# Two more raw heads loaded into an idle buffer at the start, and the first tail load moved behind the weights

## The chip, the cores and the metric

The kernel runs on one core of one Trainium2 chip. The metric is the device time of one execution in microseconds (us), the median of three runs. Three float32 modules are fused: block-causal attention, a gated two-layer block ("MoE 1") and a gated block that also mixes along the sequence ("MoE 2").

## The reference

```python
scores = 1/sqrt(64) * (q @ k.T); mask to blocks of 64: block_i >= block_j      # B=4, H=8, S=576, D=64
attn = softmax(scores);  x = attn @ v, heads side by side                      # (4, 576, 512)

xk, xr = mu*x + (1-mu)*x_prev  (one mu each; x_prev is x one step earlier)
x = sigmoid(xr @ w_r) * (relu(xk @ w_k)**2 @ w_v)                              # d_ff 1024

h = gelu(x @ w_in);  u, v = halves of h
x + (u * (w_sg @ layernorm(v) + b_sg)) @ w_out
```

## The kernel before

The function `fused_kernel` records operations on tiles; nothing is emitted while it runs. `Plan.schedule` then plays the recorded list forward several times with a table of durations (`play`, line 464), each time with other priorities, keeps the best play, and `emit` writes every engine's instructions in that order. All emitted instructions therefore carry line 670. A change to one tile or one rule can move instructions on every engine.

**Attention.** It works on 24 units for the first two batches: 16 first-kind units (`"D"`: the first 256 rows of one head, units 0 to 15) and 8 second-kind units (`"H"`: the remaining rows of two heads, units 16 to 23); the other two batches follow in the same way. A unit needs scores (tiles S0, S1, M: `S<-...` on TensorE), the softmax (row minimum and scaling on VectorE, exponential on ScalarE, tile P), transposes of P (tile T), copies of T (PH on ScalarE, PL on VectorE) and products with V (tile O). A first-kind unit loads one raw tile of 320 KB from `low`. A second-kind unit loads two raw tiles of 544 KB from `high` and one "tail" of 352 KB from `tails` (ring `tail`, one buffer), and it moves 64 KB from tile Q to tile q with a DMA (`q<-Q`) before its second score product `S<-k,q`.

**Where raw heads go.** `load` (line 909) takes a tile of `early` for the first units, and after that a tile of the ring `qkv`, which has four buffers (`RAW = 4`) and hands them out in order. `early` (lines 1482, 1483) borrows tiles of MoE 1 that are not yet in use: four heads in `kh`, four in `kl`, two in one buffer of `xh`. Units 10 to 15 go through `qkv`; a buffer of it is also used once for building mask rows. The tile `th` (ring of one) holds the tanh results of MoE 1's first part and stands empty until then.

**MoE 1** runs its products (`M<-xh,wv`: keys, then gates, then values) on TensorE between attention's. Weights arrive as raw 1024 KB tiles in the ring `w` (four buffers) and are converted by ScalarE (`wv<-w`) and VectorE (four operations each) before use; a buffer of `w` is free for the next load when its conversion is done. The first part's products on batch 1 need tile xh_515, whose fourth quarter comes from heads 14 and 15.

**The queue of loads.** SP issues all loads in order. In the planner, line 561 keeps a weight load (tag `w`) off SP while more than 4000 ns of transfers are queued; other loads are issued as they come due.

**Fillers.** Where the planner expects TensorE to idle, it inserts small matmuls on a tile of zeros (`O<-calm`) to keep the clock up; each takes TensorE's time when the gap isn't there.

Of the kernel before, what the change touches and what calls it, by code (L numbers as in the profile page):

```python
# [9 lines left out]
F32 = mybir.dt.float32  # L10
# [13 lines left out]
NL, NH, NT = 640, 1088, 704  # L24
# [40 lines left out]

FILL = 128
BACKLOG = 4000
MORE = 20.0
FILL_DUTY = 1.0
COLD_DUTY = 1.0  # L70
# [262 lines left out]
class Plan:  # L333
# [130 lines left out]
    def play(self, rings):  # L464
# [7 lines left out]
        rings16, lanes = [0.0] * 16, [-40.0] * 8  # L472
# [31 lines left out]
        def zeros(a):  # L504
            calm, op, v = self.filler.alts[0][2]["rhs"], Op(-1), a["out"]
            calm = calm.bitcast(F32) if a["lhsT"].dt == F32 else calm
            op.alts = (("tensor", "matmul", dict(out=v, lhsT=calm[:, 0:v.shape[0]], rhs=calm[:, 0:v.cols], start=False, stop=False)),)
            return op
# [9 lines left out]
        while True:  # L518
            best = None
            for e in soon:  # L520
# [3 lines left out]
                if ripe[e]:  # L524
                    t = free[e]
                elif soon[e]:
                    t = max(free[e], soon[e][0][0])
# [6 lines left out]
            t, e = best  # L534
            while soon[e] and soon[e][0][0] <= t - SLACK[e]:
                _, n, i = heapq.heappop(soon[e])
                heapq.heappush(ripe[e], (self.ops[n].p, n, i))
            if not ripe[e]:
                _, n, i = heapq.heappop(soon[e])
# [7 lines left out]
            _, n, i = heapq.heappop(ripe[e])  # L547
            if e == "PE" and STALL:
# [9 lines left out]
                    heapq.heappush(ripe[e], y)  # L558
                _, n, i = x
            op = self.ops[n]  # L560
            if e == "SP" and max(rings16) - t > BACKLOG and op.tiles and op.tiles[0].args["tag"] == "w":
                heapq.heappush(soon[e], (max(rings16) - BACKLOG, n, i))
                continue
            if e == "DVE" and len(op.alts) > i + 1 and op.alts[i + 1][0] == op.alts[i][0] and lock["POOL"] <= t:
# [20 lines left out]
            elif op.alts[i][1] == "dma_start":  # L585
# [3 lines left out]
                t = max(t, lanes.pop(0) + 40)  # L589
# [8 lines left out]
            else:  # L598
                busy, d, port = takes(e, *op.alts[i][1:])
                if e != "PE":  # L600
                    busy, d = busy + MORE, d + MORE
                s = t
                if e == "PE":
# [3 lines left out]
                    if filler and self.filler_from <= t and gap > (100 if gate.slow else 300):  # L607
                        x = gate.step(free[e])
                        more, n = filler, FILL
                        if opened:  # L610
                            more, n = zeros(group) if group["out"].cols <= FILL else None, 4 * group["out"].cols
# [123 lines left out]
def fused_kernel(ctx: ExitStack, tc: tile.TileContext, low, high, tails, mu,  # L735
# [11 lines left out]
    def pool(name, **kw):  # L747
        p = Pool(plan, name, **kw)
        return p, p
# [66 lines left out]
    mcm, mtile = pool("moe1")  # L816
# [663 lines left out]
        return t  # L1480

    early = [t[:, i] for tag in ("kh", "kl") for t in [mtile([128, 4, NL], F32, tag, 1)] for i in range(4)]
    early += [t[:, i] for tag in ("xh",) for t in [mtile([128, 2, NL], F32, tag, 2)] for i in range(2)]
    for n in range(LD0):
        load(n)
    take(loads, 1)
# [69 lines left out]
    for i, x in moe1():  # L1556
# [5 lines left out]
        i = ready  # L1562
# [328 lines left out]
    for c in range(2):  # L1891
        t = raw[c].rearrange("p (a n) -> p a n", n=HF)
# [128 lines left out]
```

## Time and profile before

| what | us |
|---|---|
| three runs | 655.10, 656.12, 656.96 |
| median | 656.12 |
| the profiled execution | 658.0 |
| its span in the trace | 656.3 |
| TensorE busy in the span | 646.5 (99%) |

The page's busy time of TensorE counts every matmul from its start to its modelled end, so short waits can be hidden in it. The trace answers say, for each engine, what ended its idle time ("waits"), list instructions in order of time ("timeline"), sum busy time in given stretches ("windows") and list DMA issues with the time to landing.

### The profile page before, as it was taken

To read this page: it belongs to the slowest core of one execution; us is meant where nothing else is said; L and a number is where in the kernel's file an instruction comes from. 1 tells how busy PE (TensorE), PEld (TensorE's weight loads), DVE (VectorE), ACT (ScalarE), POOL (GpSimd) and SP (SyncE) were. 2 spreads that over 40 slices of the span, in tenths; PEclk is the share of its full clock that TensorE was granted. 3 is DMA by queue.
4 is the path that set the end of the run, shared out by engine and by line. 5 is a ranking of instruction groups with operands and counts; after the bars stand their busy time and mean duration, and the time that the engine had idled before them with its cause. 6 is when DMAs were issued, how large, how long until landed. Compare 5 with 4: busy or idle time off the path is not lost.

```text
span 656.3 us, 12280 instructions
## 1 busy us (share of the span) xinstructions
PE 646.5 (99%) x4074; PEld 595.7 (91%) x4074; DVE 540.8 (82%) x1454; ACT 463.2 (71%) x1164; POOL 254.2 (39%) x298
## 2 busy tenths in 40 slices
PE   9989999999999999999999999999999999999997
PEld 7978778778999999999999989999898998998997
DVE  4978999988777888785897775784999999789697
ACT  6999877678966999988888976870763744534323
POOL 3033333345722457557454532440205243143054
PEclk9999999999999999999999999999999999999999
DMA  8794521333222344333343002902420440240016
GB/s 338 303 357 128 201 58 54 124 122 103 72 72 82 112 118 142 104 106 99 99 136 110 27 2 98 371 37 64 127 73 0 137 145 1 74 145 1 0 31 196
DMA packets 39615, 74.92 MB, mean 114 GB/s; under 512 B 7040, under 2 KB 22912, under 8 KB 39552
## 3 DMA queue, kind: packets, MB, share of 16 engines
q1 hardware_dynamic: 39408, 74.14, 34.3%
q8 instruction: 32, 0.52, 0.3%
q14 instruction: 31, 0.25, 0.1%
q10 hardware_dynamic: 144, 0.00, 0.0%
HBM read 62.59 MB, written 9.44 MB: 110 GB/s over the span
## 4 chain that ended last, share of the span: by engine, by line
PE 84%; ACT 7%; DMA 3%; DVE 3%; issue 1%; POOL 0%; SPq 0%; POOLq 0%; ACTq 0%; DVEq 0%
PE B L670 29%; PE M L670 26%; PE O L670 11%; PE S L670 10%; PE T L670 9%; ACT P L670 2%; DMA q<-Q 1%; ACT wv L670 1%; DMA kh<-low_dram 1%; DVE P L670 1%; DVE xT L670 1%; DMA x2d<-xh 0%; DMA o<-x2d 0%; ACT Q L670 0%; ACT PH L670 0%
## 5 line engine op out<-in xcount | busy, mean ns | idle before, releaser
L670 DVE TENSOR_TENSOR PL<-T,PH 128x384 fp32r<-128x384 f32 (+1 forms) x128 | 63.4, 504 | 32.3 <-ACT PH L670 23.0
L670 ACT ACTIVATE PH<-T 128x384 fp32r<-128x384 f32 (+3 forms) x152 | 65.8, 434 | 31.4 <-PE T L670 27.1
L670 PE MATMUL M<-xh,w 128*128 128x384 f32 (+1 forms) x272 | 75.7, 340 | 0.0
L670 PE MATMUL M<-xh,wv 128*128 128x256 f32 (+2 forms) x264 | 71.5, 359 | 0.0
L670 DVE TENSOR_SCALAR_CACHE_REDUCE P<-S 128x128 f32<-128x128 f32 (+2 forms) x124 | 58.7, 489 | 15.2 <-PE S L670 8.9
L670 ACT ACTIVATE P<-S,nb 128x128 f32<-128x128 f32 (+2 forms) x124 | 65.7, 538 | 6.4 <-DVE P L670 5.6
L670 PE MATMUL T<-ident,P 128*128 128x128 f32 x320 | 68.8, 278 | 1.3 <-DVE PL L670 0.5
L670 PE MATMUL M<-kh,wv 128*128 128x320 f32 (+2 forms) x256 | 70.0, 347 | 0.0
L670 POOL TENSOR_TENSOR Q<-qkv,Q 64x256 fp32r<-64x256 f32 x32 | 24.5, 765 | 110.8 <-ACT Q L670 80.7
L670 POOL TENSOR_TENSOR xl<-t,xh 128x384 fp32r<-128x384 f32 (+1 forms) x40 | 39.5, 995 | 50.2 <-ACT xh L670 47.7
L670 POOL TENSOR_TENSOR kl<-R,kh 128x384 fp32r<-128x384 f32 (+1 forms) x40 | 43.9, 1101 | 36.4 <-ACT kh L670 29.1
L670 PEld LDWEIGHTS T<-ident,P 128*128 128x128 f32 x320 | 42.2, 141 | 13.7 <-DVE PL L670 3.7
L670 PEld LDWEIGHTS B<-XHL,w 128*128 128x128 f32 x384 | 51.3, 188 | 0.3
L670 PE MATMUL B<-XHL,w 128*128 128x288 f32 x384 | 51.5, 294 | 0.0
L670 POOL TENSOR_TENSOR V<-qkv,V 128x320 fp32r<-128x320 f32 (+1 forms) x48 | 34.9, 737 | 38.4 <-ACT V L670 33.1
L670 PEld LDWEIGHTS M<-xh,w 128*128 128x128 f32 x272 | 48.1, 189 | 1.4
L670 PE MATMUL B<-sgh,v 128*128 128x288 f32 x224 | 49.2, 294 | 0.0
L670 PEld LDWEIGHTS M<-xh,wv 128*128 128x128 f32 x264 | 46.8, 189 | 2.6
L670 PE MATMUL M<-kl,wv 128*128 128x256 f32 (+2 forms) x160 | 48.3, 349 | 0.0
L670 PE MATMUL O<-PH,V 128*128 128x320 f32 (+3 forms) x192 | 46.5, 302 | 0.8 <-ACT PH L670 0.7
L670 PEld LDWEIGHTS M<-kh,wv 128*128 128x128 f32 x256 | 45.1, 189 | 1.9
L670 POOL TENSOR_TENSOR k<-qkv,K 64x512 fp32r<-64x512 f32 x32 | 42.6, 1331 | 7.7 <-ACT K L670 6.2
(227 smaller groups left out, 1913.6 us busy)
## 6 DMA issues: line engine op xcount, KB each, us to landing
qkv<-high_dram SPq DMA_DIRECT2D x32, 544.0 KB, 5.0
qkv<-low_dram SPq DMA_DIRECT2D x22, 320.0 KB, 3.3
tail<-tails_dram SPq DMA_DIRECT2D x16, 352.0 KB, 3.3
XHL<-x2d SPq DMA_DIRECT2D x16, 288.0 KB, 4.4
o<-x2d SPq DMA_DIRECT2D x32, 144.0 KB, 2.5
outT_dram<-o SPq DMA_DIRECT2D x32, 144.0 KB, 2.0
w<-w_k_dram SPq DMA_DIRECT2D x4, 1024.0 KB, 10.2
w<-w_v_dram SPq DMA_DIRECT2D x4, 1024.0 KB, 5.0
```

The source lines that it names most:

```text
L670: getattr(getattr(self.nc, e), fn)(*pos, **{k: real(x) for k, x in a.items() if k[0] != "_"})
```

## The change

Two edits. `early` gets a third kind of tile: one buffer of `th`, two heads wide, so that units 10 and 11 are loaded there and units 12 to 15 through `qkv`. And the planner's rule that keeps weight loads off SP while the queue is long now holds for tails too.

```diff
+GATED = ("w", "tail")
...
-            if e == "SP" and max(rings16) - t > BACKLOG and op.tiles and op.tiles[0].args["tag"] == "w":
+            if e == "SP" and max(rings16) - t > BACKLOG and op.tiles and op.tiles[0].args["tag"] in GATED:
...
-    early += [t[:, i] for tag in ("xh",) for t in [mtile([128, 2, NL], F32, tag, 2)] for i in range(2)]
+    early += [t[:, i] for tag, n in (("xh", 2), ("th", 1)) for t in [mtile([128, 2, NL], F32, tag, n)] for i in range(2)]
```

The planner's output moves on every engine. From the end backwards, the last 1552 of TensorE's 3770 matmuls stand in the same order in both (3786 after, with 16 more fillers), and so do the last 391 instructions of VectorE and the last 132 loads and stores of SP: nearly all of MoE 2. Three places follow, before and after.

SP, from the ninth load on. `low_dram` are first-kind heads, `high_dram` the large heads of second-kind units, `w_k`, `w_r`, `w_v` the weights. Before:

```order
L670 DMA xh<-low_dram 128x640 x2
L670 DMA qkv<-low_dram 128x640 x4
L670 DMA tail<-tails_dram 128x704
L670 DMA w<-w_k_dram 128x2x1024 x3
L670 DMA w<-w_r_dram 128x2x1024 x2
L670 DMA qkv<-low_dram 128x640 x2
L670 DMA qkv<-high_dram 128x1088
L670 DMA w<-w_v_dram 128x2x1024
L670 DMA qkv<-high_dram 128x1088
L670 DMA w<-w_v_dram 128x2x1024
L670 DMA q_149<-Q 64x256
```

After:

```order
L671 DMA xh<-low_dram 128x640 x2
L671 DMA th<-low_dram 128x640 x2
L671 DMA qkv<-low_dram 128x640 x4
L671 DMA w<-w_k_dram 128x2x1024 x3
L671 DMA w<-w_r_dram 128x2x1024
L671 DMA tail<-tails_dram 128x704
L671 DMA w<-w_r_dram 128x2x1024
L671 DMA qkv<-high_dram 128x1088
L671 DMA w<-w_v_dram 128x2x1024 x2
L671 DMA qkv<-high_dram 128x1088
L671 DMA q_149<-Q 64x256
```

All sixteen heads now stand ahead of the later weights, the tail stands between the two `w_r` loads, and the second large head has moved behind the second `w_v` load.

TensorE, where batch 1's keys first need the fourth quarter of xh_515 (the matmul that ends each fence; M_699 before and M_701 after are the same group, P2 and P3 are probabilities of unit 16). Before:

```order
L670 MATMUL S1_152<-tail_246 128x288
L670 MATMUL M_699<-xh_515,wv_381 128x256
L670 MATMUL M_721<-xh_515,wv_236 128x256 x2
L670 MATMUL T0_186<-ident_77,P2_643 128x128
L670 MATMUL T0_186<-ident_77,P3_649 128x128
L670 MATMUL M_721<-xh_515,wv_381 128x256
L670 MATMUL T1_194<-ident_77,P2_681 128x128
L670 MATMUL T1_194<-ident_77,P3_693 128x128
L670 MATMUL S0_132<-K_672,Q_654 128x384
L670 MATMUL S0_132<-k20_134,q20_149 128x384
L670 MATMUL M_699<-xh_515,wv_381 128x256
```

After:

```order
L671 MATMUL S1_152<-tail_422 128x288
L671 MATMUL M_722<-xh_515,wv_235 128x256
L671 MATMUL T0_185<-ident_77,P2_649 128x128
L671 MATMUL M_722<-xh_515,wv_235 128x256
L671 MATMUL M_722<-xh_515,wv_389 128x256
L671 MATMUL T0_185<-ident_77,P3_657 128x128
L671 MATMUL T1_193<-ident_77,P2_688 128x128
L671 MATMUL O0_108<-calm_73 64x128 x9
L671 MATMUL T1_193<-ident_77,P3_698 128x128
L671 MATMUL O0_108<-calm_73 64x128 x5
L671 MATMUL M_701<-xh_515,wv_389 128x256
```

The score products of unit 17 have moved behind the key product, and 14 fillers stand in front of it.

TensorE in unit 17's products with V (T1 is transposed, ScalarE copies it to PH, then `O<-PH` may start). Before:

```order
L670 MATMUL T1_194<-ident_77,P2_757 128x128
L670 MATMUL T1_194<-ident_77,P3_863 128x128
L670 MATMUL T1_194<-ident_77,Pt_875 128x128
L670 MATMUL O0_108<-PL_991,V_892 128x320
L670 MATMUL O1_240<-PL_991,V_895 128x320
L670 MATMUL S0_132<-tail_935 128x288
L670 MATMUL O0_108<-PH_1011,V_892 128x320
```

After:

```order
L671 MATMUL T1_193<-ident_77,P2_774 128x128
L671 MATMUL T1_193<-ident_77,P3_874 128x128
L671 MATMUL T1_193<-ident_77,Pt_881 128x128
L671 MATMUL S0_132<-tail_950 128x288
L671 MATMUL O0_108<-PL_1010,V_928 128x320
L671 MATMUL O1_239<-PL_1010,V_934 128x320
L671 MATMUL M_1039<-xl_285,wv_504 128x256 x2
L671 MATMUL O0_108<-PH_1037,V_928 128x320
```

Two more key products now stand between the transposes and the product that needs their copy. Counted over units 16 to 19, this step has one other product or less in between (beside the two `O<-PL`) in eight places before and in two after.

## Rows read from the trace of the kernel before

**Rows 1.** The page, busy time, share of the span and instructions of each engine.
```profile
PE 646.5 (99%) x4074; PEld 595.7 (91%) x4074; DVE 540.8 (82%) x1454; ACT 463.2 (71%) x1164; POOL 254.2 (39%) x298
```

**Rows 2.** Windows: PE, PEld, DVE, ACT, POOL busy us; granted clock; DMA share, GB/s.
```profile
0.00:60.00 60.00, 56.56 (x362) 49.08 (x363) 45.11 (x150) 51.79 (x155) 16.34 (x38) 1.00 0.82 300
60.00:160.00 100.00, 97.60 (x524) 79.50 (x523) 91.73 (x234) 79.11 (x198) 37.97 (x40) 1.00 0.34 108
160.00:400.00 240.00, 239.44 (x1536) 223.47 (x1537) 185.86 (x639) 204.52 (x581) 117.59 (x137) 1.00 0.29 89
400.00:640.00 240.00, 239.97 (x1561) 231.00 (x1560) 206.04 (x403) 121.97 (x219) 75.64 (x76) 1.00 0.28 89
```

**Rows 3.** Waits of PE, 0 to 60 us: total us, times, longest us.
```profile
PE S L670 <- DMA q<-Q: 1.2, 1, 1.2
...
PE S L670 <- DMA qkv<-low_dram: 0.6, 1, 0.6
...
PE S L670 <- ACT Pt L670: 0.2, 1, 0.2
```

**Rows 4.** Timeline of PE: start us, us taken, instruction, [idle before it <- releaser].
```profile
15.63 0.49 PE L670 MATMUL O<-calm 128*64 128x128 f32 x4
15.96 0.43 PE L670 MATMUL S<-kl 128*128 128x128 f32 x2
...
47.98 0.64 PE L670 MATMUL S<-k,q 128*128 128x384 f32 x2 [1.20 <-DMA q<-Q]
...
51.18 0.52 PE L670 MATMUL S<-k,q 128*128 128x384 f32 x1
...
57.56 0.41 PE L670 MATMUL S<-K,Q 128*128 128x384 f32 x1 [0.16 <-ACT Pt L670]
```

**Rows 5.** Timeline of SP's queue: start us, us until the last issue's end, loads.
```profile
7.44 4.59 SPq L670 DMA_DIRECT2D qkv<-low_dram  x4
12.46 0.33 SPq L670 DMA_DIRECT2D tail<-tails_dram  x1
...
19.76 10.94 SPq L670 DMA_DIRECT2D w<-w_r_dram  x2
30.79 2.08 SPq L670 DMA_DIRECT2D qkv<-low_dram  x2
...
38.42 0.33 SPq L670 DMA_DIRECT2D qkv<-high_dram  x1
39.72 0.38 SPq L670 DMA_DIRECT2D w<-w_v_dram  x1
40.19 0.52 SPq L670 DMA_DIRECT2D q<-Q  x1
...
44.22 0.47 SPq L670 DMA_DIRECT2D q<-Q  x1
```

**Rows 6.** DMA issues: first and fourth qkv, the tail, both q; us to landing last.
```profile
qkv<-low_dram SPq DMA_DIRECT2D x1, 320.0 KB, 8.3
qkv<-low_dram SPq DMA_DIRECT2D x1, 320.0 KB, 6.5
tail<-tails_dram SPq DMA_DIRECT2D x1, 352.0 KB, 7.6
q<-Q SPq DMA_DIRECT2D x1, 64.0 KB, 7.7
q<-Q SPq DMA_DIRECT2D x1, 64.0 KB, 6.8
```

**Rows 7.** Timeline of DVE, 38 to 45 us.
```profile
38.46 1.20 DVE L670 SCALAR_TENSOR_TENSOR wv<-w,wv 128x1024 int32<-128x1024 int32 x1
...
41.53 2.03 DVE L670 SCALAR_TENSOR_TENSOR xl<-xT,mu_t,xl 128x256 f32<-128x256 f32 x1
...
43.76 0.46 DVE L670 SCALAR_TENSOR_TENSOR xl<-xT,mu_t,xl 128x256 f32<-128x256 f32 x1
```

**Rows 8.** The tile th, 0 to 160 us: ns min/median/max, first to last start us.
```profile
L670 ACT ACTIVATE th<-M x4: 373/384/409, 79.3 to 92.1; 128x256 f32<-128x256 f32 x4
```

**Rows 9.** Waits of PE's weight loads, 60 to 160 us: total us, times, longest us.
```profile
PEld O L670 <- ACT PH L670: 2.4, 9, 0.3
```

## The prediction

> **What bounds the kernel now.** Read first the engines' busy time: TensorE works 646.5 us of a 656.3 us span [rows 1]. So nothing can give more than the some 10 us in which it idles, and the question is where these lie. The windows answer that [rows 2]: TensorE lacks 3.4 us of the first 60, 2.4 us of the next 100, 0.6 us from 160 to 400 and nothing from 400 to 640. Attention's start is where loads, ScalarE (51.8 of 60 us busy), VectorE and TensorE all run near their limits; later TensorE alone sets the pace. The granted clock is 1.00 in all these stretches, so no stretch is slow for its clock. In the first 60 us the waits with a name that this change can touch are 1.2 us for a `q<-Q` transfer, 0.6 us for a first-kind head and 0.2 us for ScalarE's Pt [rows 3]. Beside them stand fillers, which the page counts as busy: four of them from 15.63 to 15.96, 82 ns each [rows 4].
>
> All sums are made against the profiled execution, 658.0 us with a span of 656.3; the median of the runs is 656.1, so a difference found in the profile is put onto 656.1.
>
> **The change part by part.**
>
> *The head that came late.* The third group of loads in SP's list is held up: after the second `w_r` load is wanted, SP sits until its buffer is free, and only then, at 30.79, the last two first-kind heads go out [rows 5]. TensorE waits 0.6 us for the first of them [rows 3]. After the change these heads stand right behind the other four. The four `qkv` loads of before land at 7.44 + 8.3 = 15.7 to about 11.7 + 6.5 = 18.2 (the fourth is issued 0.33 before the group's end at 12.03), so 0.83 us apart [rows 5, 6]; six instead of four end at 19.9, ten microseconds ahead of the old issue. This wait is gone: **-0.6 us** (bounds -0.6 and 0; 0 if TensorE finds ScalarE or VectorE late instead, since both are 80 to 100% busy there).
>
> *The weights behind the heads.* The tail that made room landed at 12.46 + 7.6 = 20.1, 1.9 us after the head in front of it [rows 5, 6]; two heads take 1.7. So the `w_k` loads behind are not moved by more than -0.2 us, or +0.8 if a tail normally takes its bytes' share (352 of 320 KB, 0.9 us). Taken: **0**. Holding the tail back therefore buys the weights nothing by itself; it pays for the two heads. The four heads' 320 KB each in 0.83 us are 393 GB/s. The Trainium skill, "DMA: Bandwidth & Descriptors", section "Where 436 GB/s comes from", lets loads from HBM run at about 358 GB/s; by that figure two heads less one tail are an estimated 0.8 us more and the weights' part would read up to +0.8 instead of 0, and the sum below -0.4 instead of -1.2. The trace's rate is above it, so I keep the rows.
>
> *The tail and the borrowed tile.* SP is not made to wait for the tail: between the two `w_r` loads its queue is empty of work for 10 us anyway [rows 5]. The tile `th` is first written by MoE 1 at 79.3 us [rows 8], long after heads 10 and 11 are used up. Both cost **0**.
>
> *The q transfer.* TensorE stood 1.2 us until 47.98 for q [rows 4], which was issued at 40.19, 0.47 us behind a 1024 KB `w_v` load, and took 7.7 us to land [rows 5, 6]. Now one of the large heads, 544 KB (1.4 us at the rate above), no longer stands ahead of the first `w_v` pair, and 640 KB of first-kind heads (1.7 us) have left the stretch after 30.79. What stays ahead of q is the same list: both `w_v`, one large head. If `w_v` is issued when it was, q lands 1.2 or more earlier; if VectorE frees that buffer later, as below, q gains less. Bounds -1.2 and 0; taken **-0.8**.
>
> *The new fillers.* Two more before the first key products: 2 x 82 ns = **+0.2** (0 if the gaps are there). The 14 in front of the product that needs the fourth quarter of xh_515 are 14 x 82 ns = 1.15 us. If the gap isn't real, they are TensorE's own time; if it is, TensorE waits about as long. Before, this place cost 0.2 us [rows 3, 4], because unit 17's score products filled it. So **+1.0** (bounds +0.4, should the chain through heads 14 and 15 be so early that the planner's gap is half as long, and +2.0, should the gap be twice as long as the fillers).
>
> *From 60 to 160 us.* Weight loads of `O<-PH` waited nine times, 2.4 us in all, 0.27 each, for ScalarE's copy PH [rows 9]. That happens where hardly a product stands between the transposes and this product. The order has eight such places in units 16 to 19 before and two after, so up to 6 x 0.27 = 1.6 us can go. A load's wait is partly hidden under the running matmul (TensorE's own idle time is 2.4 us there for all causes [rows 2]), and other places become tight. Taken **-1.0** (bounds -1.6 and +1.0).
>
> *The rest.* From 160 to 400 us TensorE loses 0.6 us of 240 before; the order is new there: **0** (-0.6 to +1.0). Behind that TensorE's order is the same and it never waits: **0**.
>
> *Sum.* -0.6 + 0 - 0.8 + 0.2 + 1.0 - 1.0 + 0 = -1.2 us: 656.8 for the profiled execution, 654.9 for the median, a ratio of 0.998. Differences up to 0.3% (2.0 us) can't be told from no change, so this is "the same".
>
> **The rivals.**
>
> *Smoother all along, faster.* q no longer waits at all (-1.2), the gap at xh_515 is the short one (+0.4) and the copies PH are ahead in all six places (-1.6): -0.6 - 1.2 + 0.2 + 0.4 - 1.6 = -2.8, that is 653.3. For it: the order's looser places are countable, and the chain to xh_515 starts from heads that now land ten microseconds earlier. Against it: 14 fillers say that the planner still sees TensorE run dry.
>
> *The second `w_v` load holds the queue, slower.* Before, the second large head was issued at 38.42 and `w_v` at 39.72, as soon as VectorE's conversion ended at 38.46 + 1.20 [rows 5, 7]. Now this `w_v` stands ahead of that head and of q on SP, and its buffer depends on the same conversion; in the new order of VectorE an `xl` operation stands ahead of it. Such an operation took 0.46 us, but 2.03 in the one before that [rows 7]. With 2.03 in that place, `w_v`, the large head, both q and what follows go out 2 us later. The second q landed at 44.22 + 6.8 = 51.0 and was used at 51.18 [rows 4 to 6], with nothing to spare, so TensorE waits those 2 us. Then: -0.6 + 0 for the first q + 2.0 + 0.2 + 1.0 = +2.6, or 658.7, with nothing won later. It decides from about 1.4 us of delay on. Against it: the 2.03 us is the only such row near, and TensorE has other products to run.
>
> *The wait only moves, no change.* The early heads are not what limits the start: ScalarE and VectorE are, and what TensorE gains at 37 and 48 us it loses at xh_515, with the later stretch unchanged: -0.6 - 0.8 + 0.2 + 1.0 = -0.2, or 655.9. That the change doesn't do what it says can be left out: the loads' order shows the heads in front.
>
> **How the numbers follow.** Forecast 654.9: 36%. Only moved, 655.9: 9%. Smoother, 653.3: 34%. Held queue, 658.7, or another stretch of the new order from 60 to 400 us with waits like it: 21%. The first two lie within 0.3% of 656.1 (654.1 to 658.1): same 45%, faster 34%, slower 21%. The range reaches down past the smoother case by its remaining bounds (-0.6 in the rest, and -0.6 for the spread of the runs, 655.1 to 657.0, half of it): 652.0. Upwards it takes in the unknown +1.0 terms from 655.9 and stops short of the slow rival's middle: 658.3. Left out are some 13% above and 7% below.
>
> **What would show it.** In the trace after: no wait of S for a `low_dram` load, with the heads' last landing near 20 us; a wait of `S<-k,q` for q of at most 0.5 us near 46 us; at the fillers in front of the fourth quarter of xh_515 about 1 us between the transposes and the key product; `O<-PH` waiting some three times instead of nine from 60 to 160 us; 400 to 640 us as full as now. Wrong would be: the second `w_v` issued after 41 us, or an idle time of TensorE over 3 us between 60 and 400.

## The result: 0.5 to 0.6% slower

The changed kernel took 660.95 us (median of nine runs, 658.83 to 664.66), the kernel before 656.45 in nine runs beside it: a ratio of 1.0059, 95% interval 1.0043 to 1.0076. Compared once more (the thirteenth run) it was 1.0048 (1.0029 to 1.0066). The ratios here and below are those recorded with their intervals; they are not the quotients of the medians (1.0069 and 1.0047 for these two). The forecast of 654.9 and its range up to 658.3 were wrong, and on the wrong side. The profiled execution took 661.41 us with a span of 659.7, 3.4 more than the span before.

The page's busy time and the windows (columns as in [rows 1, 2]) of the changed kernel:

```profile
PE 648.6 (98%) x4090; PEld 598.1 (91%) x4090; DVE 546.4 (83%) x1457; ACT 461.3 (70%) x1157; POOL 254.9 (39%) x298
...
0.00:60.00 60.00, 55.65 (x350) 47.41 (x350) 44.07 (x143) 49.44 (x146) 15.83 (x37) 0.97 0.78 286
60.00:160.00 100.00, 98.91 (x538) 81.83 (x537) 92.34 (x242) 79.00 (x197) 36.10 (x37) 1.00 0.34 110
160.00:400.00 240.00, 237.96 (x1530) 222.12 (x1530) 189.65 (x640) 204.62 (x584) 122.21 (x142) 1.00 0.30 92
400.00:640.00 240.00, 239.98 (x1559) 230.91 (x1558) 205.36 (x401) 121.67 (x218) 72.45 (x74) 1.00 0.27 88
```

Of the 3.4 us, 2.1 are more busy time and 1.3 more idle time of TensorE. Against [rows 2] it lost 0.9 us before 60 us, gained 1.3 from 60 to 160, lost 1.5 from 160 to 400, and nothing behind that. A granted clock of 0.97 in the first window is new: busy time there isn't all work. The 14 fillers that now stand in front of the first product on the fourth quarter of xh_515 count as busy too. The waits (total us, times, longest), TensorE's to 60 us and from 160 to 400, its weight loads' from 60 to 160, and SP's own from 20 to 50:

```profile
PE S L671 <- DMA q<-Q: 2.8, 1, 2.8
...
PE S L671 <- ACT Pt L671: 1.6, 2, 1.4
...
PEld O L671 <- ACT PH L671: 0.8, 3, 0.3
...
SPq L671 <- PE O L671: 6.5, 2, 6.2
```

The first-kind head's 0.6 us of [rows 3] is gone. The wait for q has grown from 1.2 to 2.8, a wait of 1.4 for Pt late in the attention is new, and `O<-PH` waits three times instead of nine [rows 9]. The timeline of TensorE (start us, us, instruction, [idle before <- releaser]):

```profile
49.18 1.08 PE L671 MATMUL S<-k,q 128*128 128x384 f32 x2 [2.81 <-DMA q<-Q]
50.06 2.68 PE L671 MATMUL M<-xh,wv 128*128 128x256 f32 x6
...
60.33 0.78 PE L671 MATMUL O<-calm 128*64 128x128 f32 x9
61.03 0.33 PE L671 MATMUL T<-ident,P 128*128 128x128 f32 x1
61.12 0.54 PE L671 MATMUL O<-calm 128*64 128x128 f32 x5
61.50 0.70 PE L671 MATMUL M<-xh,wv 128*128 128x256 f32 x2
...
302.92 0.41 PE L671 MATMUL S<-K,Q 128*128 128x384 f32 x1 [1.36 <-ACT Pt L671]
```

The product that waits for q starts at 49.18, before at 47.98 [rows 4]. The six products behind it, which take 1.46 us at full clock (the first experiment shows the row), took 2.68. The granted clock says why (TensorE busy, granted clock, DMA share, GB/s):

```profile
46.00:48.00 2.00, 0.37 (x2) 1.00 0.91 309
48.00:49.00 1.00, 0.00 (x0) 1.00 1.05 400
49.00:50.00 1.00, 0.82 (x2) 0.56 0.83 335
50.00:51.00 1.00, 1.00 (x4) 0.50 0.43 136
51.00:52.00 1.00, 1.00 (x4) 0.50 0.03 8
52.00:53.00 1.00, 1.00 (x7) 0.73 0.00 0
```

After 2.8 us without work the clock stood at the lower level, 1.2 GHz, for some three microseconds, in which 1.2 us were lost on the six products and 0.4 on the pair ahead of them (1.08 against 0.64 in [rows 4]). That did not happen each time. Six of the changed kernel's sixteen executions in the two comparisons, this one among them, have a granted clock of 0.997 over the whole span (662.4 us on average); the other ten have 0.999 or 1.00 (660.1 us).

Why q is late stands in SP's timeline (start us, us to the last issue's end) and in the landings (KB, us from issue): the large head issued at 40.06, q at 40.46 and the second `w_v`, whose issue is the end of the pair at 36.11.

```profile
28.90 0.37 SPq L671 DMA_DIRECT2D w<-w_r_dram  x1
35.59 0.34 SPq L671 DMA_DIRECT2D qkv<-high_dram  x1
36.11 3.71 SPq L671 DMA_DIRECT2D w<-w_v_dram  x2
40.06 0.34 SPq L671 DMA_DIRECT2D qkv<-high_dram  x1
40.46 0.52 SPq L671 DMA_DIRECT2D q<-Q  x1
```

```profile
qkv<-high_dram SPq DMA_DIRECT2D x1, 544.0 KB, 8.7
q<-Q SPq DMA_DIRECT2D x1, 64.0 KB, 8.6
...
w<-w_v_dram SPq DMA_DIRECT2D x1, 1024.0 KB, 7.7
```

The six heads are in SBUF early, but nothing takes the place that they left. The first large head needs the ring's place of head 12, and SP waits 6.2 us for that head's last `O`: in the new order it stands 2.4 us later. TensorE's timeline, of before and then of after:

```profile
32.27 0.78 PE L670 MATMUL O<-qkv,PH 128*128 128x64 f32 x6
```

```profile
34.68 0.88 PE L671 MATMUL O<-qkv,PH 128*128 128x64 f32 x6
```

The load goes out as this ends, at 35.59 and not at 33.08. The DMA engines do nothing meanwhile (the same columns as the first windows):

```profile
34.00:36.00 2.00, 2.00 (x14) 1.63 (x14) 1.68 (x4) 2.00 (x5) 0.00 (x0) 1.00 0.00 0
```

In the kernel before their share was 1.03 here. Then `w_v`, the large head and q come all together: the head is issued at 40.06 instead of 38.42 [rows 5] and lands at 40.06 + 8.7 = 48.8 instead of 43.4, q at 49.05 instead of 47.84. What went ahead of that head landed when it had before: the first large head at 39.1, the two `w_v` at 41.7 and 47.2, against 38.9, 41.5 and 47.4. So the empty stretch used up what the early heads had given, and the second large head, now behind the second `w_v`, kept q back. ScalarE, which works in order, is held by the same loads, for 2.1 us in all:

```profile
47.21 1.12 ACT L671 ACTIVATE wv<-w 128x1024 f32<-128x1024 f32 x1 [1.63 <-DMA w<-w_v_dram]
48.76 0.42 ACT L671 ACTIVATE Q<-qkv 128x256 fp32r<-128x256 f32 x1 [0.42 <-DMA qkv<-high_dram]
```

The loss late in the attention has another cause. VectorE and GpSimd between 299 and 302.2 us (timelines of both):

```profile
299.90 2.25 DVE L671 TENSOR_TENSOR nb<-nb 128x1 f32<-128x1 f32 x1
```

```profile
299.44 0.88 POOL L671 TENSOR_TENSOR V<-qkv,V 128x320 fp32r<-128x320 f32 x1
300.27 1.02 POOL L671 TENSOR_TENSOR kl<-R,kh 128x384 fp32r<-128x384 f32 x1
301.25 0.88 POOL L671 TENSOR_TENSOR V<-qkv,V 128x320 fp32r<-128x320 f32 x1
```

A minimum of two numbers per partition, 0.16 us in the median of its sixteen, took 2.25 and ended at 302.15, 0.02 us after the last of three GpSimd operations that ran without a gap. ScalarE's Pt needs it, and TensorE's score products at 302.92 need Pt.

### The profile page after: what moved, and what is told of

Read it like the earlier page. It is cut to its first block, busy times and chain, and to the rows that moved or that the text cites. A ratio compares the mean times of both kernels' runs of the same rounds, so it can differ in the third digit from the quotient of the medians.

```text
span 659.7 us, 12297 instructions
## 1 busy us (share of the span) xinstructions
PE 648.6 (98%) x4090; PEld 598.1 (91%) x4090; DVE 546.4 (83%) x1457; ACT 461.3 (70%) x1157; POOL 254.9 (39%) x298
## 4 chain that ended last, share of the span: by engine, by line
PE 81%; DMA 6%; ACT 5%; DVE 4%; issue 1%; SPq 1%; POOL 0%; POOLq 0%
PE B L671 28%; PE M L671 26%; PE O L671 10%; PE S L671 10%; PE T L671 8%; DMA w<-w_k_dram 1%; ACT P L671 1%; DMA q<-Q 1%; DMA xh<-low_dram 1%; DMA outT_dram<-o 1%; DVE wv L671 1%; DVE P L671 1%; SPq L671 1%; ACT wv L671 1%; DMA qkv<-high_dram 1%
## 5 line engine op out<-in xcount | busy, mean ns | idle before, releaser
L671 PE MATMUL M<-kh,wv 128*128 128x320 f32 (+2 forms) x256 | 68.3, 342 | 0.0
L671 PE MATMUL O<-PH,V 128*128 128x320 f32 (+3 forms) x192 | 48.6, 308 | 0.4 <-ACT PH L671 0.2
```

The source lines that it names most:

```text
L671: getattr(getattr(self.nc, e), fn)(*pos, **{k: real(x) for k, x in a.items() if k[0] != "_"})
```

## The experiments

Their edits change the list of instructions behind the planner (`plan.order`, in which every engine finds its own order), unless another line is shown. Ratios are to the kernel before on the same chip.

**1. q by GpSimd.** Theory Q: the queue in front of q costs the time. The loop takes unit 16's two transfers.

```diff
+    for x in range(2):
+        k = place("sync", "dma_start", f"q2{x}")
+        op, _ = plan.order.pop(k)
...
+        op.alts = (("gpsimd", "tensor_copy", dict(out=a["out"].bitcast(F32R), in_=a["in_"].bitcast(F32R))),)
```

> The changed kernel, with one thing different: the two transfers of unit 16's q (64 KB each), which stood on SP behind the second w_v load and the second large head, are copies by GpSimd, right behind ScalarE's Q. The order of every other engine is that of the changed kernel. Theory Q (the queue in front of q): the 2.8 us wait of S<-k,q at 46 us is gone or under 0.8 us, the six products behind it take about 1.4 us instead of 2.7, and the time falls by 3 to 4.5 us, to 656.5 to 658 on the scale of 660.9, ratio to the kernel before 1.000 (0.998 to 1.002). Rival L (the new order from 60 us on costs the time): the wait goes, but the time stays within 1 us of the changed kernel's, ratio 1.005. Rival F (the 14 fillers in front of xh_515): likewise 1.005, with the gap in front of that product as before.

Measured: 1.0043 (1.0027 to 1.0059), a miss: some 0.7 us less than the changed kernel (1.0059 and 1.0048), not 3 to 4.5. The wait for q and the slow products are gone; the next wait has taken 0.65 us of it (TensorE's timeline):

```profile
47.33 1.46 PE L671 MATMUL M<-xh,wv 128*128 128x256 f32 x6
49.43 0.88 PE L671 MATMUL O<-qkv,PL 128*128 128x64 f32 x6 [0.65 <-ACT PL L671]
...
56.54 0.78 PE L671 MATMUL O<-calm 128*64 128x128 f32 x9
```

PL stands on ScalarE behind the copies that wait for `w_v` and the large head. The fillers' gap is still there. Another part of the miss is the price: it was read from a profile in which the clock fell. In the two profiles the product behind the fillers starts at 57.71 instead of 61.50, which is far more than the times gained. With q by GpSimd the granted clock over the span was 0.999 or 1.00 in all twelve executions, and the changed kernel's ten without the fall were about as fast as these (660.1 and 660.5 us on average, though on other chips).

**2. TensorE kept busy in the wait.** 40 fillers in front of the product that waits for q.

```diff
+    for _ in range(40):
+        plan.order.insert(k, (plan.filler, 0))
```

> The changed kernel with 40 fillers (about 3.3 us at 82 ns) on TensorE straight in front of the first S<-k,q of unit 16, the product that waits 2.8 us for q. They can't bring q any earlier. If the low clock behind the wait is a cost of its own, the six products behind it take 1.4 us instead of 2.7 at a granted clock of 1.0, and the time falls by about 1.3 us less the 0.5 us by which the fillers outlast the wait: ratio to before 1.0040 to 1.0050 instead of 1.0059. If the products behind aren't what is late (the chain through q, S and P alone sets the offset), the time is the changed kernel's plus 0 to 0.5 us, ratio 1.006 to 1.007.

Measured: 1.0041 (1.0024 to 1.0057). The six products took 1.46 us (49.96 on TensorE's timeline) at a granted clock of 1.00. The gain of 0.5 to 1.2 us is what was expected if the low clock has a cost of its own; by the interval alone it is not shown. The granted clock over the span was 0.999 or 1.00 in all twelve executions.

**3 and 4. The halves of the change alone**, each planned anew.

```diff
-GATED = ("w", "tail")
+GATED = ("w",)
```

> The first half of the change alone: heads 10 and 11 are loaded into the place of the tanh results, the tail isn't held back; the planner orders the work anew. On SP the first large head, the first w_v, the second large head and q then stand in front of the second w_v. Theory Q: q isn't behind both w_v loads and lands by 47, the wait of S<-k,q is under 1.2 us, and the time is within 1.5 us of the kernel before or below, ratio 0.997 to 1.002. Rival H (loading these heads early is what costs, by the new order from 60 us on): ratio 1.004 to 1.008, with TensorE's lost time behind 60 us.

```diff
-    early += [t[:, i] for tag, n in (("xh", 2), ("th", 1)) for t in [mtile([128, 2, NL], F32, tag, n)] for i in range(2)]
+    early += [t[:, i] for tag, n in (("xh", 2),) for t in [mtile([128, 2, NL], F32, tag, n)] for i in range(2)]
```

> The second half of the change alone: the tail is held back, heads 10 and 11 go through the ring of raw heads as before; ordered anew. On SP both large heads and both w_v loads stand alternately in front of q, as in the kernel before. Theory Q: the wait for q is 0.8 to 1.6 us and the ratio to before 0.998 to 1.002, since the weights behind the tail move by under 1 us. Rival T (holding the tail back is what costs): ratio 1.004 or more.

Measured: heads alone 1.0036 (1.0018 to 1.0053), tail alone 0.9998 (0.9981 to 1.0015). Holding the tail back costs nothing. Heads alone are slower although q stands ahead of the second `w_v`: theory Q as a matter of that one place fell, and it was open whether the early heads or the order made for them cost. The trace shows the same wait as in the changed kernel: SP stood 4.3 us until TensorE had done an `O`, the first large head was issued at 36.19 instead of 33.08, and TensorE waited up to 1.4 us for q.

**5 and 6. The minimum nb with one tensor input**, without and with the edit of q.

```diff
+    for op, _ in plan.order:
...
+            op.alts = (("vector", "tensor_scalar", dict(out=a["out"], in0=a["in0"], scalar1=a["in1"], scalar2=None, op0=a["op"])),)
```

> The changed kernel; the sixteen minima nb<-nb (128x1) that stand behind the tails' score bounds on VectorE take their second column as a scalar pointer and not as a second tensor, so each reads one tensor from SBUF. Everything else stands where it stood. In the changed kernel one of them took 2.25 us at 299.6 (median of the sixteen 0.16), ended 0.02 us after the third of three GpSimd operations that ran back to back, and a 1.36 us wait of TensorE for Pt follows; two more took 1.50 and 0.83. Theory P (VectorE is held while GpSimd runs, only where it reads two tensors of SBUF): all sixteen take under 0.3 us, the 1.36 us wait is gone, the time falls by 1 to 2 us, ratio to before 1.003 to 1.0045. Rival (the operation waits for something else, or one-input forms are held too): the same 2.25 us or so, ratio 1.005 to 1.007.

> The changed kernel with both edits: the two q transfers of unit 16 as GpSimd copies, and the minima nb with one tensor input. If the waits for q and for nb are the two largest losses and add up, the time falls by 3 us for the first (2.8 us of wait and the slow clock behind it, less what the next wait takes) and 1.3 us for the second: ratio to before 0.999 to 1.002. If the first is worth only what the first experiment's times said (about 1 us), 1.0015 to 1.0035. If neither counts, 1.005 to 1.007. The gap in front of the product that needs xh's fourth quarter, with its 14 fillers, is expected to stay.

Measured: 1.0031 (1.0017 to 1.0044) and 1.0017 (1.0005 to 1.0030), both as expected. The instructions on the tile nb in the first of the two (ns min/median/max, first to last start):

```profile
L671 DVE TENSOR_SCALAR nb<-nb x16: 197/210/216, 57.6 to 390.1; 128x1 f32<-128x1 f32 x16
```

None is held any more, and the wait for Pt at 303 us is gone. The same minimum took 2.22 to 2.25 us in each of the six traces of the new order with the new loads and two tensor inputs; with one, none of 96 in six traces took more than 0.22. The edit is worth 0.0026 and 0.0023 of the time (1.0043 to 1.0017, and 1.0054, the mean of the changed kernel's two comparisons, to 1.0031): 1.5 to 1.7 us, somewhat more than the 1.36 us of the wait. With it, q is worth 0.0014, or 0.9 us, without it 0.0011; each alone is within its intervals. The Trainium skill, "SBUF — State Buffer", section "Who interferes with whom", says that a VectorE instruction with two inputs from SBUF contends with a GpSimd instruction that reads SBUF, and that one with at most one such input, outside the modes that take two ports, does not; the 2.25 and 0.21 us agree.

**7. Two loads exchanged in the kernel before.** The second `w_v` load ahead of the second large head.

```diff
+    h = [k for k, (op, i) in enumerate(plan.order) if op.alts[i][:2] == ("sync", "dma_start")]
+    k = place("sync", "dma_start", "w", 7)
+    q = plan.order.pop(max(j for j in h if j < k))
+    plan.order.insert(k, q)
```

> The kernel before, with two of SP's loads exchanged and nothing else: the second w_v load (1024 KB) stands in front of the second large head (544 KB), as in the changed kernel. Theory Q: the head lands at 47 to 49 instead of 43.4, q 0 to 1.2 us later than 47.8; ScalarE, in order, waits for the head, TensorE's wait for q is 1.2 to 2.8 us; time up by 1 to 4 us, ratio 1.0015 to 1.006. Rival L (what costs is the new order of the compute engines, not that of the loads): ratio 0.999 to 1.001.

Measured: 1.0050 (1.0029 to 1.0071). Where that went (waits of ScalarE and of TensorE to 60 us):

```profile
ACT Q L670 <- DMA qkv<-high_dram: 3.2, 1, 3.2
...
PE M L670 <- ACT kh L670: 2.5, 1, 2.5
```

The profiled execution was the slowest of seven (663.70, their median 660.27). The head lands at 48.7, ScalarE stands 3.2 us in front of it, and TensorE waits for what stands behind on ScalarE; q, ready by then, is no longer waited for. The place of one head in the queue is worth as much as the whole loss, but by way of ScalarE.

**8. The edits of q and nb on the kernel before.**

The diffs are those of 1 and 5.

> The kernel before with the two edits of the sixth experiment: unit 16's q by GpSimd, minima nb with one tensor input. The wait of 1.2 us for q at 46.8 goes, and the nb of 0.81 us at 158. If both were on the path: 1.2 + 0.6 = 1.8 us less, ratio 0.997 to 0.999; if the next late thing (ScalarE's P, a load) takes the place of the wait: 0.999 to 1.001.

Measured: 0.9981 (0.9972 to 0.9990).

**9 and 10. The loads of the change in the old order**, without and with these edits. The table is the kernel before's own order; numbers 246 and 270 are the loads of heads 14 and 15, which go behind head 13, and 297 is the tail, which goes behind the first `w_r`.

```diff
+    plan.order = [(plan.filler if n < 0 else plan.ops[n], i) for n, i in json.loads(zlib.decompress(base64.b64decode(table)))]
...
+    move(246, 226)
+    move(270, 246)
+    move(297, 22)
```

> The loads of the change without its new order: heads 10 and 11 in the tile th, all first-kind heads in one go on SP, the tail behind the first w_r load; TensorE, VectorE, ScalarE and GpSimd do the work in the order of the kernel before, row by row. Theory Q (the early heads are worth something, and what the planner made of them costs): TensorE's 0.6 us wait for a first-kind head is gone, the large head is issued near 32.5 and lands near 36, the wait for q is at most the old 1.2 us; time down by 0.6 to 1.8 us, ratio to before 0.997 to 0.999. Rival H (the loads themselves cost, through buffers that come free later): ratio 1.002 to 1.006. If the head's wait only moves to the next late thing: 0.999 to 1.001.

> The ninth run's kernel with unit 16's q by GpSimd and the minima nb with one tensor input. If these edits add to the early heads as they add to the kernel before (0.9981): 0.9955 to 0.9975, faster than both kernels. If the early heads and the q edit remove the same lateness: 0.9975 to 0.9985.

Measured: 0.9980 (0.9967 to 0.9994) and 0.9976 (0.9963 to 0.9988). The new loads alone are worth 1.3 us by the first ratio (by the medians, 657.09 and 657.74, half of that). SP's timeline and TensorE's wait in the first of the two:

```profile
32.84 0.34 SPq L671 DMA_DIRECT2D qkv<-high_dram  x1
...
37.31 0.34 SPq L671 DMA_DIRECT2D qkv<-high_dram  x1
39.28 0.37 SPq L671 DMA_DIRECT2D w<-w_v_dram  x1
39.75 0.52 SPq L671 DMA_DIRECT2D q<-Q  x1
```

```profile
PE S L671 <- DMA q<-Q: 0.4, 1, 0.4
```

q lands at 39.75 + 6.5 = 46.2 and its wait falls from 1.2 to 0.4. The other edits then add little (0.9981 on the kernel before, 0.9976 here); q's wait is what both take away, which is the likely reason. Both kernels are faster than the two compared.

**11. PL ahead of the late head on ScalarE**, on the sixth kernel.

```diff
+    k = place("scalar", "activation", "PL", 7)
+    op, i = plan.order.pop(k)
+    plan.order.insert(max(j for j, (p, _) in enumerate(plan.order[:k]) if p.n in op.preds) + 1, (op, i))
```

> The sixth run's kernel (changed kernel, q by GpSimd, nb with one input) with one ScalarE instruction moved: PL, for which TensorE's O waits 1.06 us at 49.9, stands in front of Q and K of the large head that landed at 48.5, and not behind them. Theory S (ScalarE, in order, is held by late loads, and passes that on to VectorE and to xh's fourth quarter): the 1.06 us wait of O is under 0.3 us, what follows up to the fillers stands 0.5 to 1 us earlier; ratio to before 1.000 to 1.0010 instead of 1.0017. Rival (the 14 fillers' gap is set by VectorE's own load): 1.0015 to 1.002, the gap longer by as much.

Measured: 1.0017 (1.0003 to 1.0031), a miss. The wait is gone, and two others stand behind it, for GpSimd's part of the same late head (TensorE's timeline):

```profile
48.42 0.88 PE L671 MATMUL O<-qkv,PL 128*128 128x64 f32 x6
49.98 0.44 PE L671 MATMUL S<-K,Q 128*128 128x384 f32 x1 [0.68 <-POOL Q L671]
...
52.19 0.45 PE L671 MATMUL S<-k,q 128*128 128x384 f32 x1 [0.90 <-POOL k L671]
```

So it is the head that is late, whichever instruction shows it.

**12, 14 and 16. Without the 14 fillers**, twice on the changed kernel and once on the sixth; **13**, the changed kernel again, beside the last two.

```diff
+    fills = [k for k, (op, i) in enumerate(plan.order) if op is plan.filler]
+    for k in fills[-1:-15:-1]:
+        plan.order.pop(k)
```

> The changed kernel without the 14 fillers in front of the product that needs the fourth quarter of xh. If the gap there is real (xh ended at 61.4, M at 61.5), TensorE waits 1.0 to 1.2 us in their place, ratio to before 1.005 to 1.007 as the changed kernel's. If the fillers are TensorE's own time: 1.1 us less, ratio 1.0035 to 1.0045.

> The changed kernel as it is, on the same chip as the three that follow. If the first comparison was typical: ratio 1.005 to 1.0065, with a wait for q between 1.9 and 2.8 us. If it fell high, 1.0035 to 1.0045, and then the run without fillers had nothing to explain.

> The changed kernel without the 14 fillers, once more. If the gap is real and the fillers only fill it: the same ratio as the changed kernel beside it, within 0.001. If they are TensorE's own time: 0.0015 to 0.002 less than it.

> The changed kernel with q by GpSimd, nb with one tensor input and without the 14 fillers. If the fillers are TensorE's own time: 0.999 to 1.0005. If they fill a real gap: 1.001 to 1.002, as with the first two edits alone (1.0017). In the old order the same loads and edits gave 0.9976; what is left between the two is the price of the order by other waits.

Measured: 1.0039 (1.0026 to 1.0053) and 1.0064 (1.0048 to 1.0079) without the fillers, 1.0059 and 1.0048 with them. The means are 1.0052 and 1.0054. The traces say it more sharply. From the start of the two transposes ahead of the fillers' place to the start of the key product behind it, it takes 1.53 us in the changed kernel's first profile and 1.31 in the thirteenth run's, 1.30 and 1.53 in the two without fillers; in these two TensorE waits 0.46 us there for VectorE's P. The gap is real and the fillers cost nothing. The first of these runs alone would have said the opposite. So would the sixth kernel without fillers, which gave 1.0002 (0.9989 to 1.0014) where 1.001 to 1.002 was expected; but its gap is as long as with them (1.54 and 1.55 us). With that run, the sixth and the eleventh (1.0017 each), the order with both edits stands near 1.001, some 2 us above the old order with the same loads and edits (0.9976).

**15. The new order with the old loads.** The table is the changed kernel's order; heads 14 and 15 are loaded when heads 10 and 11 are used up.

```diff
+    move(297, 226)
+    move(246, 49, *users(139))
+    move(270, 246, *users(166))
```

> The new order without the new loads: TensorE, VectorE, ScalarE and GpSimd do the work in the order of the changed kernel, row by row, but heads 10 to 15 go through the ring of raw heads as before, the last two loaded when heads 10 and 11 are used up, the tail in its old place. If loads and order add up (loads alone 0.998, both 1.0059): 1.007 to 1.009. If the order were harmless and only its meeting with the new loads cost: 0.999 to 1.002.

Measured: 1.0141 (1.0103 to 1.0180). Loads and order don't add up:

| | old order | new order |
|---|---|---|
| old loads | 1 | 1.0141 |
| new loads | 0.9980 | 1.0059, 1.0048 |

The new order is made for the early heads (without them TensorE waits 4.4 us for one of the last first-kind heads and 2.0 for q, and the granted clock over the span was 0.995 or less in each of its six executions), and even with them it is 0.7% slower than the old one.

## Why the prediction was wrong

*The head that came late*, -0.6: right. Its wait is gone, and the ninth run shows 1.3 us for the loads in the old order, near the sum of this term and of the one for q (-1.4).

*The weights behind the heads* and *The tail and the borrowed tile*, 0: right; the tail alone gave 0.9998.

*The q transfer*, -0.8: **the step that failed**. It reads: "What stays ahead of q is the same list: both `w_v`, one large head", and it takes the bytes that left the stretch after 30.79 as time won, and beside them a large head that no longer stands ahead of the `w_v` pair. That head still stands ahead of q, behind the pair. So the list is the same, but the time isn't that of bytes. The first large head could not go before head 12 was used up, and the prediction didn't ask when the new order uses it up: 2.4 us later. The queue ran empty for over two microseconds, and the second large head went out behind the second `w_v`, landing 5.3 us later. In the old order, where the ring comes free as before, the step is right (0.4 instead of 1.2: -0.8, the ninth run). No run moved that release alone; the third (released late, q late) and the ninth (released as before, q early) bear it out in two other orders. The term came out as +1.6 in the profile, and the slow clock behind the wait, which the sum had no term for, as +1.6 more. The times say less, 0.7 to 0.9 us when q is taken off the queue: the next wait for the same loads takes part of it, and the clock fell in six of sixteen executions only.

*The new fillers*, +0.2 and +1.0: right in size. The gap is real, and without the fillers TensorE waits there for VectorE. Why VectorE is late was not tried.

*From 60 to 160 us*, -1.0: right in this profile. TensorE gained 1.3, and the copies PH are waited for three times, as counted. In the thirteenth run's profile of the same kernel they are waited for four times and the gain is 0.2 (97.83 us busy); the last section shows what else happened there.

*The rest*, 0 with bounds -0.6 and +1.0: **wrong**, +1.5. The mechanism stood in the prediction's own rows: the `xl` operation of 2.03 instead of 0.46 [rows 7] is a VectorE operation on two SBUF tensors, held from 41.53 to 43.56 while GpSimd worked without a gap (its timeline, of before):

```profile
41.19 1.27 POOL L670 TENSOR_TENSOR k<-qkv,K 64x512 fp32r<-64x512 f32 x1 [0.38 <-ACT K L670]
42.41 0.87 POOL L670 TENSOR_TENSOR V<-qkv,V 128x320 fp32r<-128x320 f32 x1
```

The prediction used it as an odd price for one place, and not as a rule that holds wherever the new order puts such an operation beside GpSimd.

Of the signs that the prediction named, those for the right steps came (the last first-kind head at 20.4 us, three waits for PH, 400 to 640 us as full), and of those for wrong ones hardly any: the second `w_v` was issued at 39.45, not after 41, and TensorE stood idle 3.13 us between 60 and 400, just over the 3 named, but 2.96 before. The sign of being right that did not come was the short wait: q was waited for 2.8 us instead of at most 0.5.

Together: -0.6 + 1.6 + 1.6 + 0.2 + 1.0 - 1.3 + 1.5 = +4.0, against 3.4 in the spans. The thirteenth run's profile, in which the clock didn't fall, gives -0.6 + 1.2 + 0.2 + 1.0 - 0.2 + 1.6 = +3.2, against 2.9 (659.2 and 656.3): other shares, and nearly the same loss. The rival "The second `w_v` load holds the queue" had the right place and the right side (658.7), but for a VectorE operation of 2.03 us that didn't come in that place: the `w_v` load was in time, and the head and q behind it were late.

What stays open: some 2 us between the two orders with q and nb mended (1.001 against 0.9976). The eleventh run shows that part of it is the late head, wherever it is waited for. The traces show a second place: from 60 to 110 us TensorE was busy for 47.2 and 47.1 of 50 us in the sixth and sixteenth runs, 49.0 in the eleventh and 49.2 in the tenth. In the first two ScalarE waited 1.7 and 1.8 us for a weight load up to 66.7 and 66.1, and VectorE was held beside GpSimd near 85 us (the last section). Each is one profile, and how the 2 us divide was not tried.

## What to carry to other kernels

Before a load that was moved forward is counted as a gain, ask what will be issued into the place that it leaves, and when the buffer for that comes free in the new order. Where a planner makes the order anew, run the new loads with the old order and the old loads with the new one: here the change itself gained 0.2% and the order that came with it lost 0.7%. And look for small VectorE operations on two SBUF tensors in a chain that others wait for; with a scalar pointer in place of the second tensor the minimum here was held in none of 96 cases. Before a wait in one profile is priced, look at how many executions have it: here the slow clock was in six of sixteen.

## What the chip showed that was not expected

VectorE was let in only when GpSimd had nothing more in a row: nb was held over the end of one GpSimd operation and two whole ones behind it (2.25 us), not just until the one that ran had ended.

Which of the two engines is held can change from one execution to the next. Here are the same two operations, started within 0.2 us of each other, in the changed kernel's first profile and in the thirteenth run's (timelines of VectorE and GpSimd):

```profile
86.26 1.21 DVE L671 SCALAR_TENSOR_TENSOR wv<-w,wv 128x1024 int32<-128x1024 int32 x1
86.24 2.38 POOL L671 TENSOR_TENSOR k<-qkv,K 64x512 fp32r<-64x512 f32 x1 [1.78 <-ACT K L671]
```

```profile
85.17 2.21 DVE L671 SCALAR_TENSOR_TENSOR wv<-w,wv 128x1024 int32<-128x1024 int32 x1
85.01 1.28 POOL L671 TENSOR_TENSOR k<-qkv,K 64x512 fp32r<-64x512 f32 x1 [1.64 <-ACT K L671]
```

Where VectorE is the one held, TensorE pays: before this pair the thirteenth run's products start 1.1 us earlier than the first profile's, and after it 0.1 us earlier. VectorE was held there (2.00 to 2.29 us) in the fifth, sixth and sixteenth runs too; in the first, second, eleventh, twelfth and fourteenth GpSimd was.

TensorE's clock did not fall after every wait. After 2.81 us the granted clock was 0.50, that is 1.2 GHz, and after 2.17 in the fourteenth run too; after 2.42 in the thirteenth it stayed at 1.00, the higher level, 2.4 GHz:

```profile
50.00:52.00 2.00, 2.00 (x13) 1.80 (x13) 1.18 (x4) 1.91 (x5) 1.93 (x2) 1.00 0.56 202
```

A transfer of 64 KB took 8.6 us to land behind 1024 and 544 KB on the same queue; the same q by GpSimd took 0.39 us.
